# A recurrent attention and a sine MLP on one core: a list scheduler's order is made anew with other operation times

## The chip, the cores and the metric

The kernel runs on one core of a Trainium2 chip. The metric is the time of one execution on the device, in microseconds (us); smaller is better. Engines are named as in the profile: PE (TensorE, matmuls), ACT (ScalarE), DVE (VectorE), POOL (GpSimd) and SP (SyncE, which here only issues DMA transfers).

## The reference

Two stages. The first is a gated linear attention: a state of 48 x 48 per head is decayed by the gate f, takes the outer product of k and v, and is read by q. The second is an MLP over the 3072 tokens with a sine in its activation.

```python
# q, k, v, f_logit: (4, 8, 768, 48)
f = 1.0 / (1.0 + np.exp(-f_logit))
for t in range(S):
    state = f[:, :, t, :, None] * state + np.einsum('bhd,bhe->bhde', k[:, :, t], v[:, :, t])
    y[:, :, t] = np.einsum('bhd,bhde->bhe', q[:, :, t], state)
# x = y as (3072, 384); w_in (384, 2048), w_out (2048, 384)
h = x @ w_in
s = np.sin(alpha * h)
g = h + s * s / (alpha + 1e-09)
return (g @ w_out).astype(np.float32)
```

## The kernel before

**Tiling.** The sequence is cut into 6 chunks c of 128 steps. A unit u = 2c + half is one chunk of two of the four batches; each unit loads f, k, q and v (384 KB each, SP's queue, three buffers per tensor). `pre(u)` makes the gates: ACT takes exp and ln of f (L328, L331), PE adds up the logs with a triangular mask (cs, L351 and L354), ACT takes two exponentials of the sums (Gi, L364, and in place, L360), and the products with k and q become one bf16 tile qk (L373: k on POOL or DVE, q on DVE); DVE casts v (vb, L335) and keeps the decay at the chunk's end (gl, L368).

**Attention.** `attend(c, b)` works on a chunk of one batch. PE transposes qk (tp, L409) and ACT or DVE copies it out (tr, L417); for chunks 4 and 5 a DMA transpose on SP's queue does both (L415). PE makes the scores (aps, L426), DVE masks them (at, L429), PE adds the old state's part and the scores' part (y, L438 and L446), ACT or DVE casts the result (yn, L452). It is transposed into xT by PE (yt, L466, copied at L469) for chunks 0 to 2 and by a DMA on SP's queue for chunks 3 to 5 (L462). The state goes on by kv (L474, L476), sum (L482) and st (L486, POOL or DVE). All PSUM tiles of this part share three buffers (ring "a").

**MLP.** `first(c, fb)` makes a block of 128 hidden units for a chunk's 512 tokens (chunk 0: two halves of 256): three matmuls into h (L543; three PSUM buffers, in chunk 0 also the two of o), Sin on ACT (L548), the square on POOL, ACT or DVE (L556, L554), and g = h + s*s/alpha on DVE (L561), which frees h. `second(c, t)` adds up 16 matmuls into o (L581; two PSUM buffers) for the 128 tokens of one batch, copies them out (osb, L589, ACT or DVE) and stores them from SP's queue (L592). An index as in h_3_13 is chunk and block; 0' marks the second half of chunk 0.

**The order.** The instructions of all engines stand in an order that a list scheduler in the kernel's own code makes at build time (`in_order`). Every operation is an `op` with a rank, a table of engines with an assumed duration in ns, dependencies and buffers. At each step the scheduler takes the operation that could start first, and the lower rank where several could. Where an operation may run on more than one engine, a number for that engine (`BIAS`, and `ON_ACT` for ACT) is added to its start before the comparison. Ranks come from `RANK`, `ATT` and `LAG` (by unit or chunk) and `KIND` (by kind of operation). Each engine then works strictly in this order.

Some orders are fixed beside it: `LOADS` is the order of the loads on SP's queue, `W_GATE` names the loads (by place in `LOADS`) whose landing lets POOL issue the two halves of w_in and then w_out, and `PHASES` orders ACT's work: the gates use the table with exp and ln, the MLP the table with Sin, and at each change ACT loads a table (L643). So ACT runs stretches: units 0 and 1, 18 Sins, units 2 and 3, 14 Sins, units 4 and 5, 10 Sins, unit 6, 6 Sins, units 7 and 8, 16 Sins, units 9 to 11, 48 Sins.

Of the kernel before, what the change touches and what calls it, by code (L numbers as in the profile page):

```python
# [22 lines left out]
LOADS = [("f", 0), ("k", 0), ("q", 0), ("f", 1), ("q", 1), ("v", 0), ("k", 1), ("v", 1), ("q", 3),  # L23
    ("f", 2), ("v", 2), ("f", 3), ("k", 4), ("q", 2), ("k", 2), ("v", 3), ("k", 3), ("f", 4),
    ("f", 5), ("v", 4), ("q", 4), ("v", 7), ("q", 5), ("f", 7), ("k", 5), ("k", 6), ("v", 5),
    ("q", 8), ("f", 6), ("f", 8), ("q", 6), ("k", 7), ("v", 6), ("k", 8), ("v", 8), ("v", 10),
    ("v", 9), ("k", 10), ("q", 7), ("f", 10), ("v", 11), ("q", 10), ("f", 11), ("k", 9), ("q",
    9), ("k", 11), ("q", 11), ("f", 9)]
W_GATE = [4, 7, 14]
LAG = [1259, 664, 156, 107, 352, 821]  # L30
ATT = [816, -410, -264, -308, -540, 67]
# [3 lines left out]
RANK = [57, 902, -416, 116, 324, -1107, 154, -228, -393, 499, -57, -21]  # L35
MULS = {"POOL": 1020, "DVE": 750}
KIND = {"v": [-253, -197, -275, -90, -19, -113, 54, -23, 294, 108, -136, 11],
        "cs": [166, -99, 466, 468, 497, 525, 156, 73, 308, 100, -174, -211],
        "kh": [-420, -288, -109, -60, -261, -416, 1, 112, -116, -353, -597, -410],
        "qh": [39, -59, -267, -207, -95, -105, -79, -204, -36, -58, 106, 145],  # L40
        "tp": [-704, -587, -407, -250, -350, -423, -529, -434, -209, -113, -630, -619],
        "tr": [676, 683, 605, 574, 597, 434, 658, 637, 516, 502, 841, 893],
        "a": [-193, -33, -307, -268, -491, -499, -415, -297, -236, -148, -542, -369],
        "m": [382, 244, 882, 926, 455, 521, 870, 880, 558, 664, 209, 409],
        "y": [359, 281, 782, 934, 738, 726, 967, 789, 882, 759, 797, 900],
        "yt": [338, 442, 591, 498, 369, 453, 920, 776, 936, 571, 725, 839],
        "xe": [164, 118, 474, 430, 628, 568, 660, 448, 819, 638, 731, 791],
        "i": [-178, -9, -130, -85, -385, -454, -347, -676, -80, 105, -145, 51],
        "kv": [105, 140, -54, 56, 130, -66, -209, -24, 56, 108, 260, 93],
        "st": [-156, -144, -34, 68, -433, -296, -147, -222, -33, 60, -123, -22],  # L50
        "h": [-282, -193, -192, -427, -22, -104, -640, -227, -306, -284, -211, -314],
        "sq": [110, -5, -368, -360, -77, -233, -538, -538, -402, -388, -227, -18],
        "g": [-196, -86, -99, -320, -310, -185, -65, -203, 63, 30, -333, -448],
        "ev": [98, 89, -544, -601, -357, -242, -98, -190, -420, -283, -225, -463]}
ON_ACT = {"tr": [164, -107, -316, 43, -634, 114, -467, 93, 3854, -711, -8369, -5250],
          "y": [-1550, -3600, -3600, -14550, -10950, -650, 1050, -4550, -350, -5050, 3650, 100],
          "xe": [5550, 6200, -5450, 2700, 200, -100, 4250, 6900, 4000, 6850, 2600, 2800],
          "sq": [200, 900, 10400, -1400, -450, 450, -100, -1000, -250, 7250, -250, 12600],
          "ev": [7850, 12700, 3150, 2350, 850, 50, -5400, -700, 3000, 9250, 8600, -1850]}
BIAS = {"ACT": 500, "DVE": 500, "POOL": 600, "SP": 200}  # L60
# [98 lines left out]
def kernel(  # L159
# [45 lines left out]
    PE, ACT, DVE, POOL, SP = "PE", "ACT", "DVE", "POOL", "SP"  # L205
# [4 lines left out]
    EXP, TRIG = "natural_log_exp_and_others", "trig_and_small"  # L210
# [6 lines left out]
    def op(rank, engs, emit, deps=(), takes=(), holds=(), table=None, dma=None):  # L217
        o = Op(rank, engs, emit, [d for d in deps if d is not None], list(takes), table, dma)
        for b in list(takes) + list(holds):
            b.users.append(o)  # L220
        ops.append(o)
        return o

    R = {n: Ring(b) for n, b in dict(
        f=3, k=3, q=3, v=3, lf=2, qk=NQ, vb=NV, gl=6, Gi=4, a=N_A, tr=4, at0=3, at1=3, xT=2,
# [96 lines left out]
    def pre(u, rank):  # L322
# [15 lines left out]
        l = op(rank, {ACT: 790}, ln_, deps=[x], takes=[lf], holds=[fb_], table=EXP)  # L338
        act = [x, l]
        made["v", u] = op(rank + KIND["v"][u] + 2, {DVE: 870}, values, deps=[vb_.ready], takes=[vv], holds=[vb_])  # L340
        late = []
        for i in range(2):
# [34 lines left out]
            c_ = op(rank + KIND["cs"][u] + i, {PE: 170 if last else 370}, cs_, deps=[l], takes=[cb], holds=[lf])  # L377
# [8 lines left out]
            made["qh", m] = op(rank + KIND["qh"][u] + i, {DVE: 490}, qm, deps=[g, qb_.ready], takes=[qkb], holds=[qb_, cb])  # L386
            if not last:
                made["gl", m] = op(rank + i, {DVE: 110}, gl_, deps=[g], takes=[glb], holds=[cb])
# [3 lines left out]
    def attend(c, b, rank):  # L392
# [35 lines left out]
        def m_(e, r):  # L428
            nc.vector.tensor_mul(tl[x, "at", r], tl[x, "a"][r], mask4)  # L429
# [59 lines left out]
        if c < PE_TR:  # L489
            kt = op(rank + KIND["tp"][u], {PE: 250}, lambda e: tp_(e, 0), deps=[made["kh", m]], takes=[tpb], holds=[qkb])  # L490
            qt = op(rank + KIND["tp"][u], {PE: 250}, lambda e: tp_(e, 1), deps=[made["qh", m], kt], holds=[tpb, qkb])
            tr = op(rank + KIND["tr"][u], {DVE: 640, ACT: 970}, tr_, deps=[qt], takes=[trb], holds=[tpb])
            tr.on_act = ON_ACT["tr"][u]
        else:
            tr = op(rank, {SP: 1300}, tr_, deps=[made["kh", m], made["qh", m]], takes=[trb], holds=[qkb], dma=3000)
        a = op(rank + KIND["a"][u], {PE: 400}, a_, deps=[tr], takes=ab + atb, holds=[trb])
        ms = [op(rank + KIND["m"][u], {DVE: 640}, lambda e, r=r: m_(e, r), deps=[a], holds=[ab[r], atb[r]]) for r in range(2)]
        last_ = None
        if not first:
            last_ = op(rank + KIND["i"][u], {PE: 210}, inter_, deps=[a, made["st", c - 1, b]], takes=[yb], holds=[trb, sold])  # L500
        for r in range(2):
            last_ = op(rank + KIND["i"][u], {PE: 170}, lambda e, r=r: intra_(e, r), deps=[ms[r], last_, made["v", u]],
                       takes=[yb] if first and r == 0 else [], holds=[yb, atb[r], vb])
        y_op = op(rank + KIND["y"][u], {DVE: 520, ACT: 430}, y_, deps=[last_], takes=[ynb], holds=[yb])
        y_op.on_act = ON_ACT["y"][u]
        if c < Y_TR:
            yt = op(rank + KIND["yt"][u], {PE: 200}, yt_, deps=[y_op], takes=[ytb], holds=[ynb])
            made["x", c, b] = op(rank + KIND["xe"][u], {DVE: 300, ACT: 440}, x_, deps=[yt], takes=[xb], holds=[ytb])
            made["x", c, b].on_act = ON_ACT["xe"][u]
        else:  # L510
            made["x", c, b] = op(rank + KIND["xe"][u], {SP: 1300}, yt_, deps=[y_op], takes=[xb], holds=[ynb], dma=1200)
        if not last:
            sold_op = made.get(("st", c - 1, b))
            if c < SUM:
                kv = op(rank + KIND["kv"][u] + 1, {PE: 200 if first else 370}, kv_, deps=[made["kh", m], made["v", u], sold_op],
                        takes=[kvb, sb], holds=[qkb, vb] + ([sold] if sold else []))
                made["st", c, b] = op(rank + KIND["st"][u] + 1, {DVE: 520}, st_, deps=[kv, made["gl", m]],
                                      holds=[sb, kvb, bufs["gl", m]])
            else:
                kv = op(rank + KIND["kv"][u] + 1, {PE: 200}, kv_, deps=[made["kh", m], made["v", u], sold_op],  # L520
                        takes=[kvb, sumb, sb], holds=[qkb, vb])
                su = op(rank + KIND["st"][u] + 1, {DVE: 520}, sum_, deps=[kv, sold_op], holds=[sumb, kvb, sold])
                made["st", c, b] = op(rank + KIND["st"][u] + 1, {POOL: 800, DVE: 710}, st_, deps=[su, made["gl", m]],
                                      holds=[sb, sumb, bufs["gl", m]])
            bufs["st", c, b] = sb


    def first(c, fb, ts, rank, needs):
# [39 lines left out]
        s = op(rank, {ACT: 455 if half else 645}, sin_, deps=[a, made["al"]], takes=[sb], holds=[hb], table=TRIG)  # L568
        t = op(rank + KIND["sq"][w], {POOL: 640 if half else 1040, ACT: 420 if half else 640, DVE: 520 if half else 917}, sq, deps=[s], takes=[s2b], holds=[sb])
        t.on_act = ON_ACT["sq"][w]  # L570
        made["g", c, fb, ts.start] = op(rank + KIND["g"][w], {DVE: 420 if half else 685}, add, deps=[t], takes=[gb], holds=[s2b, hb])
        return s

    def second(c, t, rank):
# [18 lines left out]
        v_ = op(rank + KIND["ev"][2 * c + t // 2], {DVE: 520, ACT: 500}, ev, deps=[prev], takes=[sbuf], holds=[ob])  # L593
# [81 lines left out]
```

## Time and profile before

| | |
|---|---|
| median of 7 runs | 220.29 us (219.09 to 220.7) |
| the profiled execution, in all | 218.93 us |
| its span, first to last instruction | 217.2 us |
| busy PE / DVE / ACT / POOL | 180.9 / 160.2 / 163.4 / 100.0 us |
| mean granted TensorE clock | 0.958 |
| DMA moved | 30.30 MB |

The costliest groups of the profile, each with its operation, count, busy time, mean of one, and idle time of the engine before them:

```profile
L556 POOL TENSOR_TENSOR s<-s 128x512 f32<-128x512 f32 (+1 forms) x67 | 58.5, 888 | 67.9 <-ACT s L548 46.9
L543 PE MATMUL h<-xT,w_in_bf 128*128 128x512 bf16 (+1 forms) x336 | 78.3, 358 | 10.1 <-DMA w_in_bf<-in_moe_w_in_dram 5.3
L548 ACT ACTIVATE s<-h,al_p 128x512 f32<-128x512 f32 (+1 forms) x112 | 67.4, 626 | 25.2 <-PE h L543 21.7
L561 DVE SCALAR_TENSOR_TENSOR g<-s,al_r,h 128x512 bf16<-128x512 f32 (+1 forms) x112 | 72.0, 666 | 10.2 <-POOL s L556 6.5
L581 PE MATMUL o<-w_out_bf,g 128*128 128x384 bf16 x384 | 78.4, 329 | 0.0
```

Matmuls overlap each other, so 329 ns is how long one o matmul takes from start to end, not how far apart they stand. No engine is full over the whole span, and where each is full differs by stage; the stages are the stretches of ACT between its table loads. In the span's 40 slices each digit is a busy share in tenths, and a slice is 5.43 us.

### The profile page before, as it was taken

The numbers are of one execution on the slowest core, as the hardware profiler recorded it, in microseconds if no ns is written. First come the engines' busy times: TensorE is split into PE (matmuls) and PEld (weight loads), VectorE is DVE, ScalarE is ACT, GpSimd is POOL, SyncE is SP. The second block draws the span as 40 slices with busy tenths as digits, with TensorE's granted clock in tenths as the row PEclk, the third lists the DMA queues.
The fourth block names the chain that finished last, engine by engine and source line by source line (L and its number), as shares of the span: only waits on it lengthen the run. The fifth ranks groups of instructions, "written<-read, shape, count | busy, mean of one in ns | idle before, by whom it ended". The sixth has DMA issues, their size and how long they took to land.

```text
span 217.2 us, 4284 instructions
## 1 busy us (share of the span) xinstructions
PE 180.9 (83%) x1537; PEld 107.3 (49%) x1537; DVE 160.2 (74%) x297; ACT 163.4 (75%) x269; POOL 100.0 (46%) x129
## 2 busy tenths in 40 slices
PE   0468628546999979896999979998999999999993
PEld 0337515335676654463665535554554555555561
DVE  2386864657689589988969997759999968787820
ACT  3565535996579987798998898997898888687601
POOL 5332534767352378856675725378504213203200
PEclk9999995965899999999999999999999999999999
DMA  7999999999999999969939999586201211001121
GB/s 130 188 187 197 190 186 197 188 208 216 213 160 198 188 166 202 180 120 210 191 82 145 186 188 196 144 170 147 69 15 41 92 54 41 0 36 72 38 74 72
DMA packets 118997, 30.30 MB, mean 139 GB/s; under 512 B 113072, under 2 KB 118208, under 8 KB 118976
## 3 DMA queue, kind: packets, MB, share of 16 engines
q1 hardware_dynamic: 115968, 26.88, 71.5%
q0 software_dynamic: 3008, 3.15, 9.2%
q8 instruction: 12, 0.20, 0.4%
q14 instruction: 9, 0.07, 0.1%
HBM read 25.17 MB, written 4.72 MB: 138 GB/s over the span
## 4 chain that ended last, share of the span: by engine, by line
PE 52%; ACT 13%; DVE 9%; DMA 8%; POOL 6%; SPq 5%; issue 5%; ACTq 0%; POOLq 0%
PE o L581 23%; PE h L543 22%; SPq L270 5%; DMA v<-in_v_dram 5%; DVE g L561 4%; POOL s L556 4%; DMA w_in_bf<-in_moe_w_in_dram 3%; ACT L643 3%; ACT s L548 3%; ACT Gi L364 2%; DVE at L429 2%; PE aps L426 2%; ACT lf L331 1%; ACT f L328 1%; PE tp L409 1%
## 5 line engine op out<-in xcount | busy, mean ns | idle before, releaser
L556 POOL TENSOR_TENSOR s<-s 128x512 f32<-128x512 f32 (+1 forms) x67 | 58.5, 888 | 67.9 <-ACT s L548 46.9
L543 PE MATMUL h<-xT,w_in_bf 128*128 128x512 bf16 (+1 forms) x336 | 78.3, 358 | 10.1 <-DMA w_in_bf<-in_moe_w_in_dram 5.3
L548 ACT ACTIVATE s<-h,al_p 128x512 f32<-128x512 f32 (+1 forms) x112 | 67.4, 626 | 25.2 <-PE h L543 21.7
L561 DVE SCALAR_TENSOR_TENSOR g<-s,al_r,h 128x512 bf16<-128x512 f32 (+1 forms) x112 | 72.0, 666 | 10.2 <-POOL s L556 6.5
L581 PE MATMUL o<-w_out_bf,g 128*128 128x384 bf16 x384 | 78.4, 329 | 0.0
L543 PEld LDWEIGHTS <-w_in_bf 128*128 128x128 bf16 x336 | 32.8, 101 | 36.4 <-issue 7.5
L581 PEld LDWEIGHTS <-g 128*128 128x128 bf16 x384 | 35.7, 98 | 23.5 <-issue 0.5
L429 DVE TENSOR_TENSOR at<-aps,mask 128x512 bf16<-128x512 f32 x48 | 31.7, 684 | 4.4 <-PE aps L426 4.2
L373 POOL TENSOR_TENSOR qk<-k,Gi 128x384 bf16<-128x384 f32 x22 | 21.9, 1012 | 21.2 <-ACT Gi L364 18.8
L373 DVE TENSOR_TENSOR qk<-q,cs 128x384 bf16<-128x384 f32 x24 | 13.1, 552 | 12.8 <-ACT cs L360 12.2
L554 ACT ACTIVATE s<-s 128x512 f32<-128x512 f32 (+1 forms) x34 | 20.8, 614 | 0.9
L351 PE MATMUL cs<-lf,mask 128*128 128x384 bf16 x24 | 8.1, 357 | 9.9 <-ACT lf L331 8.5
L446 PE MATMUL y<-vb,at 128*128 128x48 bf16 x192 | 11.5, 187 | 4.9 <-DVE vb L335 3.0
L409 PE MATMUL tp<-ident,qk 128*128 128x128 bf16 x128 | 12.2, 258 | 3.3 <-POOL qk L373 1.9
L446 PEld LDWEIGHTS <-at 128*128 128x128 bf16 x192 | 8.9, 98 | 11.1 <-DVE at L429 5.2
L643 ACT ACT_TABLE_LOAD x11 | 14.1, 1283 | 0.2
L328 ACT ACTIVATE f<-f 128x768 f32<-128x768 f32 x12 | 10.1, 838 | 5.0 <-DMA f<-in_f_logit_dram 4.9
L426 PE MATMUL aps<-tr 64*128 64x128 bf16 x192 | 11.2, 230 | 2.4 <-ACT tr L417 1.5
L364 ACT ACTIVATE Gi<-cs 128x384 f32<-128x384 f32 x24 | 11.6, 485 | 1.9 <-PE cs L354 1.9
L417 ACT COPY tr<-tp 128x1024 bf16<-128x1024 bf16 x10 | 9.9, 1019 | 3.9 <-PE tp L409 3.9
L556 DVE TENSOR_TENSOR s<-s 128x512 f32<-128x512 f32 (+1 forms) x11 | 7.8, 709 | 6.8 <-ACT s L548 6.6
L409 PEld LDWEIGHTS <-qk 128*128 128x128 bf16 x128 | 10.4, 117 | 4.9 <-POOL qk L373 2.6
(54 smaller groups left out, 155.3 us busy)
## 6 DMA issues: line engine op xcount, KB each, us to landing
f<-in_f_logit_dram SPq DMA_DIRECT2D x12, 384.0 KB, 7.0
k<-in_k_dram SPq DMA_DIRECT2D x12, 384.0 KB, 6.5
q<-in_q_dram SPq DMA_DIRECT2D x12, 384.0 KB, 6.8
v<-in_v_dram SPq DMA_DIRECT2D x12, 384.0 KB, 6.8
out_dram<-osb SPq DMA_DIRECT2D x24, 192.0 KB, 2.0
w_in_bf<-in_moe_w_in_dram POOLq DMA_DIRECT2D x6, 256.0 KB, 6.6
w_out_bf<-in_moe_w_out_dram POOLq DMA_DIRECT2D x4, 384.0 KB, 6.5
xT<-yn SPq DMA_TRANSPOSE x12, 2.4
```

The lines of the kernel that those rows point to most:

```text
L364: nc.scalar.activation(out=tl["Gi", m], in_=tl["cs", m][:, :H * D], func=Act.Exp)
L373: engine[e].tensor_mul(qk_b[bufs["qk", m].place % NQ][:, "kq".index(n), :, :, :D], tl[n, u][:, i * H:(i + 1) * H, :].rearrange("c (r p) d ...
L409: nc.tensor.transpose(tl[x, "tp"][:, j * HP + p, :], qk_b[qkb.place % NQ][:, j, p, :, :].rearrange("c r e -> c (r e)"), ident)
L429: nc.vector.tensor_mul(tl[x, "at", r], tl[x, "a"][r], mask4)
L446: nc.tensor.matmul(tl[x, "y"][:, h * D:(h + 1) * D], tl[x, "at", r][:, p, :], v_b[vb.place % NV][:, i, h, :], start=(first and p == r == 0 ...
L543: nc.tensor.matmul(h[:, :n], w_in_bf[:, kb, fs], xT[:, ts.start // C:ts.stop // C, kb, :], start=(kb == 0), stop=(kb == KB - 1))
L548: nc.scalar.activation(out=s[:, :n], in_=tl[x, "h"][:, :n], func=Act.Sin, scale=al_p[:, fb:fb + 1])
L554: nc.scalar.activation(out=s2[:, :n], in_=s[:, :n], func=Act.Square)
L556: engine[e].tensor_mul(s2[:, :n], s[:, :n], s[:, :n])
L561: nc.vector.scalar_tensor_tensor(tl["g", c, fb][:, ts], tl[x, "s2"][:, :n], al_r[:, fb:fb + 1], tl[x, "h"][:, :n], Alu.mult, Alu.add)
L581: nc.tensor.matmul(tl["o", c, t], tl["g", c, fb][:, t * P:(t + 1) * P], w_out_bf[:, fb, :], start=(fb == 0), stop=(fb == FB - 1))
L643: nc.scalar.preload_act_table_set(now)
```

## The change

All durations that the scheduler assumes are set to other values, and with them all of its other numbers: the loads' order, the gates' places, the ranks and the per-engine numbers. No operation is added, removed or altered, `PHASES` stays, and the values computed stay the same. What changes is the order of the instructions on each engine and, for operations that have a choice, the engine.

```diff
-LOADS = [("f", 0), ("k", 0), ("q", 0), ("f", 1), ("q", 1), ("v", 0), ("k", 1), ("v", 1), ("q", 3),
-    ("f", 2), ("v", 2), ("f", 3), ("k", 4), ("q", 2), ("k", 2), ("v", 3), ("k", 3), ("f", 4),
-    ("f", 5), ("v", 4), ("q", 4), ("v", 7), ("q", 5), ("f", 7), ("k", 5), ("k", 6), ("v", 5),
-    ("q", 8), ("f", 6), ("f", 8), ("q", 6), ("k", 7), ("v", 6), ("k", 8), ("v", 8), ("v", 10),
-    ("v", 9), ("k", 10), ("q", 7), ("f", 10), ("v", 11), ("q", 10), ("f", 11), ("k", 9), ("q",
-    9), ("k", 11), ("q", 11), ("f", 9)]
-W_GATE = [4, 7, 14]
-LAG = [1259, 664, 156, 107, 352, 821]
-ATT = [816, -410, -264, -308, -540, 67]
+LOADS = [("f", 0), ("k", 0), ("q", 0), ("f", 1), ("v", 0), ("q", 1), ("k", 1), ("v", 1), ("f", 3),
+    ("k", 3), ("q", 3), ("f", 2), ("q", 2), ("k", 4), ("k", 2), ("v", 3), ("v", 2), ("f", 4),
+    ("q", 4), ("f", 5), ("q", 5), ("k", 5), ("v", 4), ("v", 7), ("v", 5), ("k", 6), ("f", 6),
+    ("k", 7), ("q", 8), ("f", 7), ("q", 6), ("k", 8), ("f", 8), ("v", 6), ("v", 8), ("v", 9),
+    ("v", 10), ("k", 9), ("q", 7), ("k", 10), ("f", 11), ("f", 9), ("q", 11), ("q", 9), ("q",
+    10), ("k", 11), ("f", 10), ("v", 11)]
+W_GATE = [5, 7, 14]
+LAG = [1394, 1064, 594, 47, 278, 1466]
+ATT = [814, -396, -222, -531, -395, 119]
...
-        "y": [359, 281, 782, 934, 738, 726, 967, 789, 882, 759, 797, 900],
+        "y": [-24, 45, 570, 660, 439, 417, 826, 557, 855, 722, 643, 734],
...
-BIAS = {"ACT": 500, "DVE": 500, "POOL": 600, "SP": 200}
+BIAS = {"ACT": 400, "DVE": 500, "POOL": 600, "SP": -12300}
...
-        l = op(rank, {ACT: 790}, ln_, deps=[x], takes=[lf], holds=[fb_], table=EXP)
+        l = op(rank, {ACT: 840}, ln_, deps=[x], takes=[lf], holds=[fb_], table=EXP)
...
-            tr = op(rank + KIND["tr"][u], {DVE: 640, ACT: 970}, tr_, deps=[qt], takes=[trb], holds=[tpb])
+            tr = op(rank + KIND["tr"][u], {DVE: 670, ACT: 1010}, tr_, deps=[qt], takes=[trb], holds=[tpb])
...
-        a = op(rank + KIND["a"][u], {PE: 400}, a_, deps=[tr], takes=ab + atb, holds=[trb])
+        a = op(rank + KIND["a"][u], {PE: 345}, a_, deps=[tr], takes=ab + atb, holds=[trb])
...
-        t = op(rank + KIND["sq"][w], {POOL: 640 if half else 1040, ACT: 420 if half else 640, DVE: 520 if half else 917}, sq, deps=[s], takes=[s2b], holds=[sb])
+        t = op(rank + KIND["sq"][w], {POOL: 640 if half else 1040, ACT: 420 if half else 640, DVE: 470 if half else 820}, sq, deps=[s], takes=[s2b], holds=[sb])
...
```

`RANK`, the other rows of `KIND`, all of `ON_ACT` and the remaining durations change in the same manner. The number of `BIAS` for SP has no part in any comparison, since no operation has SP beside another engine.

## The prediction

> **What bounds the kernel now.** I read the page's slices first, to see which engine is full where. The kernel alternates between two ACT tables, so I then cut the span at ACT's table loads, taken from ACT's timeline, and asked for the busy time of each engine in each piece. The waits, the chain that ended last and the SP queue came last.
>
> ```profile
> PE   0468628546999979896999979998999999999993
> DVE  2386864657689589988969997759999968787820
> ACT  3565535996579987798998898997898888687601
> 40.14:48.39 8.25, 4.10 (x37) 2.67 (x36) 3.88 (x8) 8.03 (x14) 5.22 (x8) 0.83 1.38 198
> 48.39:66.85 18.46, 16.31 (x181) 11.93 (x182) 14.57 (x31) 12.35 (x23) 10.04 (x16) 0.80 1.16 200
> 66.85:77.20 10.35, 10.35 (x104) 6.64 (x101) 7.08 (x19) 10.16 (x17) 2.74 (x5) 1.00 1.26 188
> 77.20:90.87 13.67, 11.61 (x132) 6.49 (x131) 13.22 (x22) 10.44 (x17) 12.31 (x13) 1.00 1.14 183
> 113.36:133.15 19.79, 17.96 (x146) 9.31 (x144) 18.62 (x32) 16.98 (x28) 10.65 (x12) 1.00 1.34 183
> 133.15:144.70 11.55, 11.29 (x88) 6.41 (x87) 7.52 (x15) 11.37 (x21) 6.42 (x7) 1.00 0.62 149
> 144.70:217.20 72.50, 67.66 (x461) 36.10 (x459) 53.16 (x81) 51.48 (x82) 20.21 (x21) 0.99 0.22 61
> ```
>
> Columns of the cut: stretch, length, busy PE, weight loads, DVE, ACT, POOL, clock, DMA share, GB/s. Three regimes stand out. Up to 34 us the second half of w_in is awaited. From 40 to 145 us ACT is nearly full: its gaps lie in the Sin stretches, while the Exp stretches (40 to 48, 67 to 77, 133 to 145) have none. From 149 us PE is full:
>
> ```profile
> 146.77 0.27 PE L446 MATMUL y<-vb,at 128*128 128x48 bf16 x4 [0.51 <-DVE at L429]
> 149.11 0.81 PE L543 MATMUL h<-xT,w_in_bf 128*128 128x512 bf16 x3 [0.25 <-DVE g L561]
> 204.07 9.60 PE o L581 x59
> ACT s L548 <- PE h L543: 21.7, 40, 5.0
> DVE g L561 <- POOL s L556: 6.5, 17, 1.1
> 125.60 1.97 SPq L270 DMA_DIRECT2D f<-in_f_logit_dram  x1
> 127.66 3.22 SPq L415 DMA_TRANSPOSE tr<-qk  x1
> 132.86 5.43 SPq L462 DMA_TRANSPOSE xT<-yn  x4
> ```
>
> The matmul at 149.11 is h_3_3, the fourth first-layer block of chunk 3. The chain ends with 59 matmuls in 9.60 us, so one o costs 0.163 us; three h matmuls cost 0.65 (start to start in PE's timeline). Likewise a transpose costs 0.054, a score matmul (aps) 0.042, a y or kv matmul about 0.03 to 0.042. With these, 63.6 us of PE work stand from h_3_3 on, and 213.7 - 149.1 = 64.6 us pass. So the end is the start of h_3_3 plus the PE work that is left, and h_3_3 starts 4.4 us after the last table load at 144.70. That load is set by ACT's stretches before it.
>
> **What the Trainium skill says.** "ScalarE: Activation LUTs", What ACT_TABLE_LOAD costs, gives 1283 ns for a load and a drain of about 1380 ns. The trace has 1283 ns (x11) and the next activation 10 ns later: no drain is charged. "SBUF — State Buffer", Who interferes with whom, says that a DVE cast in a two-port mode and a POOL operation block each other fully. The trace agrees: the values' cast (L335, 0.56 us at best) at 47.13 took 2.25 us while POOL ran two products. "TensorE: Matmul & The Clock Gate", What's actually happening, says that PE's clock falls to half after an idle window: the granted clock is 0.50 from 50 to 55 us, after the thin stretch from 40. "Perfetto Trace Analysis", DMA Instruction — HWDGE, says that the record of a DMA instruction ends before the data has moved: an SP load shows about 2 us, but lands 6.5 to 7.0 us after its issue.
>
> **The change, part by part.** No operation is added or removed. By the instruction order of both programs, three tr copies go from DVE to ACT (3 x 1.02 = +3.1 us ACT, 3 x 0.685 = -2.1 DVE), two k products from DVE to POOL (2 x 1.012 against 2 x 0.837), and one or two squares, xT, st and osb change sides. ACT: +0.48 (osb), +0.42 (square), -0.48 (xT); in all 171.9 to 175.4 us by row means, which count overlaps twice. DVE: about -3.0. PE's 161 us stays as it is.
>
> *0 to 40 us.* v_1 stays the eighth load, so its landing, the POOL gate behind it (23.8 us) and the landing of w_in's second half (33.9) stay. On PE kv_0_2 now stands ahead of aps_0_2 and needs v_1, so h_0_0 starts near 26.6 instead of 21.7. The eight Sins before the second half take 8 x 0.42 plus a table load and yn and end near 34: covered by that landing, but with nothing left over. After it POOL's squares set the pace (9 in 5.64 us); now 8 are POOL's and 2 ACT's, and ACT's 12 x 0.42 = 5.0 becomes the pace: -0.5 us (between 0 and -0.7).
>
> *Sin stretch from 48.* DVE takes gl_6 and a q product before the values' cast, which frees PSUM for the next transposes about 1.5 us earlier (PE waited until 50.54 for this). But 11.3 us of PE work stand between h_0_5 and h_0_15 instead of 9.5, and ACT has a tr and a yn more (12.6 to 13.2). I carry -0.5; bounds 0 and -2.
>
> *Exp stretch from 67.* Two tr and a yn leave ACT (2 x 0.97 + 0.38), two xT come in (2 x 0.38), and h_1_0 waits for these xT, the cs behind it for 0.35 us: -1.1, carried -1.6.
> *Sin stretch from 77.* Its ACT work rises from 11.1 to 12.6 us. Each Sin waits for an h, that for one of three PSUM buffers, freed by g: 10 Sins in 12.4 us. The 2.6 us of ACT gaps take part of the 1.6 us; +0.9, carried -0.7. In the short Exp stretch from 91, cs_12 stands behind h_1_12 in both orders: carried -0.5.
> *Sin stretch from 97.* POOL now has st_2_0, a product, a square, st_2_1 and only then the next squares; DVE's square there is gone. One st (0.85) comes into the loop: +0.9, carried +0.4.
> *Exp stretch from 104.* tr_3_2 leaves ACT (about -0.7), cs_15 and cs_17 come behind h_2_0 to h_2_2, which wait for the last xT_2 (+0.3): carried 0.
> *Sin stretch from 113.* ACT +0.9 (tr_3_3 and an osb in, a square out), DVE 20 us in 21 in both. Bounds -0.3 and +1.2; I take +0.5.
> *Exp stretch from 133.* A yn leaves (-0.4). But SP's order has changed: k_10, f_11, f_9, q_11, q_9, q_10, k_11, f_10 and v_11 stand in one row, and k_10 needs the buffer of k_7, free near 112. Nine loads at 2.07 us (384 KB at 185 GB/s) end at 131 to 133; before there were seven, from 113.5 to 127.6. tr_4_0 (issued at 112.2 before), tr_4_1 and two xT_3 stand behind them, so aps_4_0 starts near 136, with PE waiting up to 3 us; the cs behind it is still in time. h_3_0 then starts near 140, and 3 h, 13 o and two cs (4.4 us) stand before cs_23: the last Gi comes about 0.4 us late. Net 0 (between -0.4 and +1.8), carried +0.5.
>
> *The end.* Ahead of h_3_3 PE had 97.3 us of work; now 95.7, because 188 instead of 192 o matmuls, and one batch less of chunk 4's scores (8 matmuls) and y products (16), stand there: 4 x 0.163 + 8 x 0.042 + 0.6 = 1.6 us move behind h_3_3. From h_3_13 on both orders are the same (108.8 us of work ahead, 212 o). Between these two points before had 12.0 us for 11.5 of work; now 13.1 of work needs about 13.3: +1.3. Two st on POOL stand ahead of the first square, against a DVE wait that they replace: +0.1.
>
> Sum: +0.5 + 1.3 + 0.1 = +1.9 us on a span of 217.2. The profiled execution took 218.93 in all, 1.36 under the median of 220.29; added to both, 220.8 and 222.2.
>
> **The rivals.**
> Faster. The Exp stretch from 67 hands on its 1.1 us whole, because the lighter DVE (21.0 instead of 22.4 us up to g_1_9) lets the loop run while ACT takes the tr copies in its gaps, and the stretch from 48 gives 0.9. Then the last table load comes at -0.5 - 0.9 - 1.1 - 0.4 = -2.9; plus 1.4 at the end: -1.5 us, 218.8; with ACT's gaps closed further, 216.5. It decides once the load comes before 143.3 (144.70 - 1.4). For it: ACT idles 5.9 us in the stretch from 48 and DVE is full from 77. Against it: the three h buffers set that pace, and the tr go into the same in-order queue as the Sins.
> No change. The deferred o fall into PE's gaps before h_3_3 (0.51, 0.15, 0.25 us there) and the stretches come out even: 220.3. Against it: 1.6 us is more than these gaps.
> Slower by the load row. If k_10's buffer comes 1 us later, or the transposes drain slower, v_11's cast (ahead of g_2_13 on DVE) and aps_4_0 pass the time at which cs_18 is due, and ACT waits up to 1.8 us: 224.0.
> That the new order doesn't take effect is out: the programs differ on all five engines.
>
> **How the numbers follow.** Forecast, 221.3 to 223.2: 0.33, at 222.2. Load row, 223.2 to 226: 0.14. No change, within 1.1 us of 220.3: 0.19. Faster, 216.5 to 219.2: 0.34. Within 0.5% is about what a measurement of this kernel can't tell from no change. So faster 0.34, same 0.19, slower 0.47. Cut to four fifths, the range is 217.4 to 224.4; the likeliest case alone has 221.3 to 223.2.
>
> **What would show it.** The last table load between 144.5 and 146 and h_3_3 4.5 us behind it; about 13.3 us from h_3_3 to h_3_13; the Exp stretch from 67 shorter by a microsecond and the next Sin stretch longer; a PE wait for tr near 133. A load before 143.3 makes me wrong, as does a PE that was never full behind h_3_3.

## The result and the profile after

| | before | after |
|---|---|---|
| median of the runs | 219.77 us (57 runs, 217.35 to 221.23) | 220.46 us (22 runs, 219.33 to 222.11) |
| ratio after / before | | 1.0053, 95% interval 1.0032 to 1.0075 |
| the profiled execution | 218.93 us | 221.25 us |
| its span | 217.2 us | 219.6 us |

The ratio is taken over fast runs alone, that is without those over 1.5% above the fastest of the same kernel, which are 9 of the 57 of the kernel before and none of the kernel after. The change costs 0.7 us by the medians of all runs, and about 1.2 us (half a per cent) by the ratio. Slower was the likeliest side; the size, 222.2 us, was not met. The two profiled executions lie 2.32 us apart, twice what the ratio says. That gap has to be explained too.

The clock's row of the page's slices, first of the kernel before (a slice is 5.43 us), then of the kernel after (5.49 us); a digit is a tenth:

```profile
PEclk9999995965899999999999999999999999999999
PEclk9999999757999999976999999999999999999999
```

In both the clock falls somewhere between 38 and 60 us. The kernel before had a dip in slice 7 too (32.6 to 38 us), which is gone; the dip in slices 18 and 19 (93 to 104 us) is new. Next, the kernel after, cut at its own table loads (stretch, length, busy PE, weight loads, DVE, ACT, POOL, clock, DMA share, GB/s):

```profile
27.29:38.81 11.52, 9.32 (x72) 6.26 (x72) 9.31 (x21) 10.35 (x25) 7.79 (x13) 1.00 1.14 192
47.06:64.33 17.27, 16.33 (x190) 11.61 (x189) 14.23 (x30) 12.81 (x23) 10.22 (x16) 0.86 1.13 197
64.33:73.39 9.06, 7.86 (x64) 4.56 (x63) 5.19 (x14) 8.79 (x16) 3.79 (x4) 1.00 1.20 188
73.39:87.20 13.81, 12.40 (x143) 7.50 (x142) 12.57 (x22) 11.73 (x17) 10.57 (x12) 1.00 1.13 185
93.07:104.41 11.34, 8.64 (x77) 5.25 (x75) 9.32 (x15) 7.48 (x10) 8.43 (x9) 0.70 0.83 140
104.41:112.67 8.26, 6.17 (x62) 3.32 (x59) 6.00 (x14) 8.04 (x14) 5.01 (x6) 1.00 0.33 100
112.67:133.79 21.12, 20.11 (x156) 10.99 (x153) 19.75 (x32) 17.99 (x28) 10.07 (x10) 1.00 1.25 188
133.79:145.28 11.49, 10.74 (x82) 5.88 (x83) 7.20 (x15) 11.08 (x19) 6.00 (x7) 1.00 0.75 147
```

In the same view of the kernel before, the end of its first Sin stretch, the six Sins, and the Exp stretch behind them:

```profile
33.94:40.14 6.20, 5.54 (x28) 3.97 (x29) 4.18 (x9) 4.52 (x10) 4.37 (x8) 0.61 1.20 183
96.53:104.19 7.66, 5.96 (x63) 3.52 (x62) 6.70 (x11) 6.92 (x10) 5.37 (x6) 1.00 1.04 211
104.19:113.36 9.17, 9.17 (x103) 5.79 (x100) 7.26 (x17) 8.95 (x14) 5.98 (x7) 1.00 0.61 123
```

Set side by side, the starts of the table loads (in us) give a ledger. The last column is the forecast's carried sum.

| ACT's table load | before | after | difference | forecast |
|---|---|---|---|---|
| Exp, units 2 and 3 | 40.14 | 38.81 | -1.33 | -0.5 |
| Exp, units 4 and 5 | 66.85 | 64.33 | -2.52 | -0.5 |
| Sin (10 Sins) | 77.20 | 73.39 | -3.81 | -1.6 |
| Sin (6 Sins) | 96.53 | 93.07 | -3.46 | -0.5 |
| Exp, units 7 and 8 | 104.19 | 104.41 | +0.22 | +0.4 |
| Sin (16 Sins) | 113.36 | 112.67 | -0.69 | 0 |
| Exp, units 9 to 11 | 133.15 | 133.79 | +0.64 | +0.5 |
| Sin (last) | 144.70 | 145.28 | +0.58 | +0.5 |
| start of h_3_3 | 149.11 | 150.23 | +1.12 | +0.6 |
| end of the last o | 213.66 | 215.99 | +2.33 | +1.9 |

The last three rows are near the forecast, but the way there isn't. Up to 93 us the new order gains 3.5 us, and in the stretch of six Sins it loses 3.7. PE's timeline of the kernel after shows that place (start, duration, operation, tile, count, idle time and what ended it):

```profile
93.77 0.34 PE L466 MATMUL yt<-ident,yn 128*128 128x128 bf16 x3
96.01 0.48 PE L426 MATMUL aps<-tr 64*128 64x128 bf16 x8 [1.90 <-ACT tr L417]
97.29 1.44 PE L543 MATMUL h<-xT,w_in_bf 128*128 128x512 bf16 x3 [0.80 <-DVE g L561]
98.52 0.53 PE L581 MATMUL o<-w_out_bf,g 128*128 128x384 bf16 x1
98.84 1.06 PE L409 MATMUL tp<-ident,qk 128*128 128x128 bf16 x8
...
102.58 1.02 PE L543 MATMUL h<-xT,w_in_bf 128*128 128x512 bf16 x3
104.89 0.34 PE L581 MATMUL o<-w_out_bf,g 128*128 128x384 bf16 x1 [0.35 <-DVE g L561]
```

PE waits 1.90 us for tr_3_0, whose copy stands on ACT behind the table load and a Sin, and then 0.80 for g_1_10. From 97.3 to 102.6 matmuls take nearly twice their time (three h 1.44 us instead of 0.81, eight tp 1.06 instead of 0.61), and the granted clock of that window is 0.50. The kernel before waited for tr_3_0 too, 1.46 us, and then 0.24 for g, and its clock stayed at 1.00 (the line of 96.53). So the question was whether the fall is the loss or only comes with it.

### The profile page after: what moved, and what is told of

It is laid out like the page before. It is cut to its first block, busy times and chain, and to the rows that moved or that the text cites. A ratio compares the mean times of both kernels' runs of the same rounds, so it can differ in the third digit from the quotient of the medians.

```text
span 219.6 us, 4261 instructions
## 1 busy us (share of the span) xinstructions
PE 184.4 (84%) x1537; PEld 108.7 (50%) x1537; DVE 158.3 (72%) x293; ACT 166.7 (76%) x273; POOL 100.5 (46%) x129
## 4 chain that ended last, share of the span: by engine, by line
PE 56%; DMA 15%; DVE 9%; ACT 7%; SPq 4%; issue 4%; POOL 3%; DVEq 0%; ACTq 0%; POOLq 0%
PE h L543 24%; PE o L581 23%; DMA k<-in_k_dram 9%; SPq L270 4%; DVE g L561 4%; DMA w_in_bf<-in_moe_w_in_dram 3%; DMA w_out_bf<-in_moe_w_out_dram 3%; POOL s L556 2%; PE aps L426 2%; ACT L643 2%; PE y L446 2%; ACT s L548 2%; DVE vb L335 1%; DVE qk L373 1%; PE tp L409 1%
## 5 line engine op out<-in xcount | busy, mean ns | idle before, releaser
L556 POOL TENSOR_TENSOR s<-s 128x512 f32<-128x512 f32 (+1 forms) x66 | 57.1, 875 | 74.2 <-ACT s L548 54.1
L543 PE MATMUL h<-xT,w_in_bf 128*128 128x512 bf16 (+1 forms) x336 | 80.0, 360 | 8.1 <-DVE g L561 5.1
L373 POOL TENSOR_TENSOR qk<-k,Gi 128x384 bf16<-128x384 f32 x24 | 23.8, 1014 | 20.8 <-ACT Gi L364 19.8
L351 PE MATMUL cs<-lf,mask 128*128 128x384 bf16 x24 | 8.8, 377 | 11.0 <-ACT lf L331 9.7
L417 ACT COPY tr<-tp 128x1024 bf16<-128x1024 bf16 x13 | 13.0, 1013 | 4.9 <-PE tp L409 4.9
L368 DVE TENSOR_TENSOR gl<-cs,bd 128x8 f32<-128x8 f32 x20 | 3.2, 161 | 18.5 <-ACT cs L360 18.4
L452 ACT CAST yn<-y 128x384 bf16<-128x384 f32 x17 | 8.1, 477 | 6.7 <-PE y L446 6.6
```

The source lines that it names most:

```text
L373: engine[e].tensor_mul(qk_b[bufs["qk", m].place % NQ][:, "kq".index(n), :, :, :D], tl[n, u][:, i * H:(i + 1) * H, :].rearrange("c (r p) d ...
L543: nc.tensor.matmul(h[:, :n], w_in_bf[:, kb, fs], xT[:, ts.start // C:ts.stop // C, kb, :], start=(kb == 0), stop=(kb == KB - 1))
L556: engine[e].tensor_mul(s2[:, :n], s[:, :n], s[:, :n])
```

## The experiments

Theory A says that PE's clock, falling behind the new wait, makes the loss of the six-Sin stretch and decides how long an execution takes. Theory B says that the order of DVE and POOL there (casts of v and a state product ahead of squares) makes it. For the end the theory is the prediction's: PE is full from h_3_3 on. All repeats below write the same values once more, so nothing is left out of the computation.

Where an experiment moves an operation, the scheduler's finished order is taken, and `moved` puts one operation right ahead of or behind another; everything else stays in its place:

```diff
-    for o, e in in_order(ops, {"table": act_order, "load": load_order, "h": h_order, "cs": cs_order}):
+    todo = in_order(ops, {"table": act_order, "load": load_order, "h": h_order, "cs": cs_order})
+    for what, ahead in MOVES:
+        todo = moved(todo, what, ahead)
+    for o, e in todo:
```

**The changed kernel again (after_again).** The same kernel once more.

> The changed kernel as it is. Theory A (clock): between 93 and 104 us PE idles 1.9 and 0.8 us in front of aps_3_0 and h_1_13, and in a part of the executions its clock then falls to half for some 6 us; so the executions fall into two groups, mean clock near 0.975 with a span near 218.2 us and near 0.960 with a span near 219.6, and the median lies between, 220.1 to 220.7 us. Theory B (order of DVE and POOL): the 3.7 us lost in that stretch come from casts and state products ahead of the squares and are there in every execution; spans then don't follow the clock.

Six runs: 221.35 us median (220.14 to 222.24), above the 220.1 to 220.7 that was expected. Each execution has its mean clock on record. All executions of the two kernels that have one, sorted by it (medians in us):

| mean clock | before (168 executions, three sessions) | after (28 executions) |
|---|---|---|
| 0.972 and more | 7, median 217.4 | 11, median 219.96 |
| 0.966 to 0.971 | 16, 219.4 | 5, 220.6 |
| 0.956 to 0.965 | 86, 219.24 | 12, 221.47 |
| less | 59, 220.56 | none |

The changed kernel takes 1.5 us more where its mean clock is near 0.960 than where it is near 0.975. Both profiled executions of the kernel after (0.960) show the fall at 97. The profile of before (0.958) lies below its median by 0.84 us. The table also shows what the mean clock alone does not explain: in each of the three rows that both kernels have, the new order is the slower one, by 1.2 to 2.6 us, and it has no execution in the lowest row, where the old one has 59 of 168.

**PE kept busy in the wait (warm97).**

```diff
-            for kb in range(KB):
+            for kb in list(range(KB)) * REPEAT.get((c, b), 1):
                 nc.tensor.transpose(tl[x, "yt"][:, kb, :], tl[x, "yn"][:, kb, :], ident)
+REPEAT = {(2, 2): 12}
```

> The changed kernel with the three transposes of yt_2_2 issued 12 times instead of once (the same values written again), 33 more of 0.054 us = 1.8 us of PE work in the place where PE waited 1.90 us for tr_3_0. Theory A: the clock stays at 1.00 in that stretch, every execution has a mean clock of 0.974 or more, the stretch from the table load near 93 to the next takes about 9.3 us instead of 11.3, and the median is 0.4 to 0.9 us under that of the changed kernel. Theory B: no gain, 0 to +0.5 us.

220.01 us median (218.35 to 221.19, 22 runs), ratio to before 1.0028 (1.0004 to 1.0051). The 28 executions of the kernel after have a median of 220.62. No execution fell below a mean clock of 0.969 (theory A expected 0.974; six lie at 0.969). Its cut and PE's timeline:

```profile
93.50:102.17 8.67, 7.59 (x101) 5.42 (x101) 8.44 (x14) 7.38 (x10) 7.66 (x9) 1.00 0.70 131
102.17:111.66 9.49, 7.71 (x66) 4.02 (x66) 6.52 (x15) 8.23 (x14) 5.88 (x7) 0.82 0.52 146
```

```profile
94.20 2.18 PE L486 MATMUL yt<-ident,yn 128*128 128x128 bf16 x36
97.73 0.81 PE L574 MATMUL h<-xT,w_in_bf 128*128 128x512 bf16 x3 [0.89 <-DVE g L592]
103.70 0.34 PE L614 MATMUL o<-w_out_bf,g 128*128 128x384 bf16 x1 [0.76 <-DVE g L592]
106.28 1.44 PE L574 MATMUL h<-xT,w_in_bf 128*128 128x512 bf16 x3 [0.19 <-DVE xT L489]
```

The stretch shrinks from 11.34 to 8.67 us with the clock at 1.00: of the 3.7 us lost there, 2.7 were the clock. But the next stretch grows from 8.26 to 9.49, since now the clock falls at 106, behind waits much like those that the kernel after had there without a fall. Theory A holds for the place; the fall was moved, not removed.

**The order of DVE and POOL (order97).**

```diff
+MOVES = [(("v", 6), ("behind", ("at", 3, 0, 1))),
+         (("v", 8), ("behind", ("g", 1, 13))),
+         (("st", 2, 1), ("behind", ("sq", 1, 12)))]
```

> The changed kernel with the casts of v_6 and v_8 behind at_3_0 and g_1_13 on DVE (they stood ahead of g_1_10) and st_2_1 behind the square of h_1_12 on POOL. Theory B: the stretch from 93 gets 1 to 2 us shorter and the time falls by 0.7 us or more. Theory A: g_1_10 comes at most 0.35 us earlier, the clock still falls in a part of the executions, and the time moves by 0 to -0.4 us.

224.85 us (223.04 to 225.69, 6 runs), ratio 1.0265 (1.0207 to 1.0323): a miss for both theories. Three lines from SP's, DVE's and PE's timelines suggest why:

```profile
83.75 16.70 SPq L288 DMA_DIRECT2D v<-in_v_dram  x4
109.13 0.56 DVE L625 COPY osb<-o 128x384 f32<-128x384 f32 x1 [2.39 <-DMA out_dram<-osb]
110.01 1.44 PE L575 MATMUL h<-xT,w_in_bf 128*128 128x512 bf16 x3 [2.22 <-DVE xT L490]
```

In the kernel after the same four v loads are through in 11.63 us. The cast of v frees the buffer that a later v load waits for. Put 5 us later, it holds up SP's queue and the stores behind the loads. The copy of o then waits for a store buffer, the copy of xT stands behind it on DVE, and h_2_0 waits for xT. This chain is read from the timelines; the three moves were not made one by one. The six-Sin stretch itself was 1.2 us shorter (94.05 to 104.19), as theory B expected, but its clock was 0.83 instead of 0.70, so the run doesn't part the two theories there. It says nothing of the state product alone either.

**The state product alone (st21),** on warm2_o13 below: only the last of these three moves.

> warm2_o13 with st_2_1 behind the square of h_1_12 on POOL, alone. The prediction's step (one state product of 0.85 us in the loop of the six Sins costs 0.9): the stretch from the table load near 93, 8.7 us in warm2_o13, gets 0.4 to 0.9 us shorter, and the median falls by 0.2 to 0.8 us from 217.97. Theory A (that stretch lost its time to the clock, POOL had slack): the stretch stays within 0.2 us and the median within 0.3.

218.13 us (22 runs) against 217.97 in an earlier session; the stretch takes 8.67 us against 8.68. The state product ahead of the squares costs nothing there. What the casts cost at full clock, no run tests.

**The end (o13_early).**

```diff
+MOVES = [(("osb", 2, 2), ("before", ("sum", 4, 2)))]
+MOVES += [(("o", 1, 3, i), ("before", ("aps", 4, 1))) for i in range(5)]
+MOVES += [(("o", 1, 3, i), ("before", ("h", 3, 3))) for i in range(12, 16)]
```

> The changed kernel with the copy of o_2_2 ahead of the sums of chunk 4 on DVE, five o_1_3 matmuls ahead of aps_4_1 and the last four o_1_3 ahead of h_3_3, so that 192 and not 188 o matmuls stand ahead of h_3_3. Theory (PE is full from h_3_3 on, so what stands behind it adds its own length): 4 x 0.163 = 0.65 us plus the gaps of 0.73 and 0.47 us that are filled ahead of it, so -0.6 to -1.2 us. Rival (the loop of Sin, square and g sets the pace from 149 to 162, PE has slack there): 0 to -0.2 us.

219.69 us (22 runs), ratio to before 1.0019 (0.9993 to 1.0044), 0.77 us under the kernel after. From the last table load to the end it takes 69.95 us (145.61 to 215.56), after 70.71, before 68.96. PE's timeline there:

```profile
145.60 0.50 PE L504 MATMUL kv<-vb,qk 128*128 128x96 bf16 x8
145.94 0.98 PE L622 MATMUL o<-w_out_bf,g 128*128 128x384 bf16 x5
146.84 0.58 PE L454 MATMUL aps<-tr 64*128 64x128 bf16 x8
150.44 0.81 PE L582 MATMUL h<-xT,w_in_bf 128*128 128x512 bf16 x3
```

Five o fill what was a wait of 0.48 and 0.25 us ahead of aps_4_1, h_3_3 stays 4.8 us behind the load, and four o fewer behind it take 0.64 us off the way to h_3_13 (12.53 against 13.17). So PE's work behind h_3_3 adds its own length, as the prediction said of the end, and the rival (PE has slack there) is out.

**Both places kept busy, and all together (warm2, warm2_o13).** warm2 adds to warm97 the wait that took the fall over:

```diff
-            for p in range(HP):
+            for p in list(range(HP)) * AGAIN.get((c, b), 1):
                 for r in range(2):
+AGAIN = {(3, 1): 3}
+REPEAT = {(2, 2): 12, (2, 3): 4}
```

> The changed kernel with the filling of warm97, and also aps_3_1 issued three times instead of once (16 more of 0.042 us = 0.67) and yt_2_3 four times (9 more of 0.054 = 0.49), ahead of the waits between 102 and 106. In the profile of warm97 the clock no longer fell at 97 but at 106.3 (six h and cs there at half speed), which gave back some 1.2 us. Theory A: this fall goes too, mean clock 0.980 or more, last table load about 1 us earlier than in warm97 (143.5), median 218.6 to 219.4. Rival: the second fall was paid for by waiting ACT anyway, or the time is lost again behind 113: the median stays at 219.7 to 220.3.

> warm2 and the moved o_1_3 of o13_early in one kernel. If the two losses lie in different places they add: 0.6 to 0.8 us under warm2, 218.0 to 218.8, faster than both kernels. If the end gains only what the clock fall left it, it equals warm2.

warm2: 218.5 us (22 runs), 0.9979 (0.9955 to 1.0003). warm2_o13: 217.97 us (217.27 to 218.63, 22 runs), 0.9948 (0.9928 to 0.9969), better than either kernel as it stands. warm2, cut as above:

```profile
93.38:102.05 8.67, 7.59 (x101) 5.42 (x101) 8.44 (x14) 7.37 (x10) 7.66 (x9) 1.00 0.72 134
102.05:110.31 8.26, 7.15 (x92) 4.62 (x92) 6.55 (x15) 8.04 (x14) 5.66 (x7) 1.00 0.51 150
110.31:131.46 21.15, 20.13 (x157) 11.12 (x154) 19.39 (x32) 17.97 (x29) 10.08 (x10) 1.00 1.20 183
```

Both stretches now run at full clock, in the profile; 14 of the 22 executions have a mean clock of 0.982 or more. The last table load comes at 143.06, 2.2 us ahead of the kernel after, and all of it reaches the end (213.77 against 215.99). The clock's falls between 93 and 110 thus cost the new order some 2 us in such an execution.

**The early fall (warm3).** warm2_o13 with the same kind of repeats between 40 and 48 us:

```diff
+MORE = {(0, 20): 5, 5: 6, 6: 5}
+TWICE = {(1, 1, 1): 5}
```

> warm2_o13 with PE filled also between 40 and 48: h_0_4 of the second half issued five times, cs_5's and cs_6's large matmul six and five times, the last four transposes of tp_1_1 five times (the same values again; about 3.6 us of PE work in waits of 1.3, 0.9, 1.2 and 1 us). Theory: the clock no longer falls between 45 and 51, where some 3 us of PE work ran at half speed; the table load near 64.6 comes 0.3 to 1.3 us earlier, the median is 0.2 to 1.0 us lower than 217.97, mean clock 0.985 or more. Rival (ACT and the loads set that stretch): the median stays within 0.2 us, or rises where a repeat delays a copy.

217.72 us (22 runs), 0.9954 (0.993 to 0.9978). The mean clock of its profiled execution is 1.00, and 0.994 or more in all 22. The stretch of 14 Sins, first in warm2_o13 and then in warm3:

```profile
47.18:64.58 17.40, 16.38 (x190) 11.30 (x189) 14.13 (x30) 12.64 (x23) 10.19 (x16) 0.90 1.28 205
```

```profile
47.77:63.99 16.22, 16.07 (x206) 11.53 (x205) 14.21 (x30) 12.53 (x24) 10.15 (x16) 1.00 1.27 211
```

The stretch is 1.2 us shorter. (That it starts 0.6 later comes from ahead of the repeats: ACT's first load for Sin stands at 28.01 against 27.43.) The last o end 0.6 us earlier, 212.22 against 212.82. The medians differ by 0.25 us, which the intervals don't tell from nothing.

**The same for the kernel before (before_warm).** tp_3_1's last four transposes seven times, in front of its own 1.46 us wait near 99.

> The kernel before the change with the last four transposes of tp_3_1 issued seven times (24 more of 0.054 us = 1.3), in the place where its PE waited 1.46 us for tr_3_0 near 99. The executions of the kernel before fall into groups too: about a third at a mean clock of 0.951 or less (median 220.5), the others at 0.961 (219.2) and above. Theory: the lowest group is the clock falling behind that same wait, so it becomes rare, and the median falls by 0.2 to 0.6 us, to about 219.1 to 219.4. Rival: the lowest group falls somewhere else; its share stays near a third and the median at 219.7.

219.89 us (22 runs), ratio 1.0012 (0.9982 to 1.0041); 8 of 22 executions still had a mean clock below 0.956. A miss: with this wait filled, the lowest clock group stays as frequent as it was (59 of 168), so it comes from somewhere else. A kernel before with the thin stretch from 40 to 50 us filled too, expected at 217.1 to 217.7, was tried twice and gave no measurement. So whether the old order gains as much as the new one stays open; its 7 executions at 0.972 and more (median 217.4) hint that it does.

**The gate of w_in (gate0_v0).**

```diff
-        return op(rank, {POOL: 100}, lambda e: nc.gpsimd.tensor_copy(seen[:, i:i + 1], tl[n, u][0:1, 0, 0:1]),
+        return op(rank, {POOL: 100}, lambda e: nc.gpsimd.tensor_copy(seen[:, i:i + 1], (tl[n, u] if i else tl["v", 0])[0:1, 0, 0:1]),
```

> The changed kernel with every engine's order as it is, only the copy on POOL that opens the first half of w_in waits for v_0, the fifth load, as the fifth load opened it before, and not for q_1, the sixth. Theory: what moved the start is this gate: with it on the fifth load, v_1 comes behind the three w_in parts again, the second gate opens at 21.5 to 23.8 us instead of 19.6, the second half of w_in lands some 2 to 4 us later and the Exp table load now at 38.8 to 39.1 comes at 39.8 to 40.5; the time rises by 0.3 to 1.2 us. Rival (the order of the loads itself, not the gate): the second gate and that table load stay within 0.3 us, and the earlier first half brings 0 to -0.5 us.

220.35 us (13 runs), ratio 1.0059 (1.0029 to 1.0088), no different from the kernel after. POOL's and PE's timelines:

```profile
21.93 0.56 POOL L302 COPY seen<-v 1x1 f32<-1x1 f32 x1 [2.90 <-DMA v<-in_v_dram]
23.93 1.12 POOL L309 DMA_DIRECT2D w_in_bf<-in_moe_w_in_dram  x2
```

```profile
31.58 3.77 PE L573 MATMUL h<-xT,w_in_bf 128*128 128x256 bf16 x24 [0.45 <-DVE g L591]
```

The second gate opens 2.3 us later than in the kernel after (19.62), as expected, and still the second half of w_in lands before the h that need it: they wait for g, and the Exp load comes at 38.26, earlier than 38.81, where 39.8 to 40.5 was expected. So a gate at 21.9 costs the new order nothing. That isn't yet the 23.8 of the kernel before, which no run restores.

**A copy on DVE instead of ACT (tr33_dve),** on warm2_o13: tr_3_3 as in the kernel before.

> warm2_o13 with the copy tr_3_3 on DVE (0.67 us) and not on ACT (1.0 us), at the same place of the order, as the kernel before had it. The stretch of 16 Sins from the load near 110 took 21.1 us against 19.8 in the kernel before. If ACT's extra work sets it, it gets 0.5 to 1.0 us shorter and the median 0.4 to 1.0 us lower; if DVE, busy 19.5 of these 21 us, sets it, the median rises by 0.1 to 0.6 us.

218.36 us (22 runs), 0.4 us over warm2_o13 in its earlier session. The stretch of 16 Sins, first in warm2_o13 and then here:

```profile
110.24:131.38 21.14, 20.13 (x157) 11.13 (x154) 19.66 (x32) 17.96 (x28) 10.07 (x10) 1.00 1.19 186
110.13:131.85 21.72, 20.30 (x157) 11.12 (x154) 20.80 (x33) 17.16 (x27) 10.44 (x10) 1.00 1.21 186
```

The stretch gets 0.58 us longer as 1.1 us of busy time goes to DVE and 0.8 leaves ACT: DVE sets this stretch, and moving the copy to ACT was right.

## Why the prediction was right on the side and wrong on the size

**The step that failed most** is "*Sin stretch from 97* ... One st (0.85) comes into the loop: +0.9". The stretch lost 3.68 us. 2.7 of them are PE's clock (warm97: 8.67 us at full clock). The last 1.0 us over before's 7.66 is near the forecast's size, but st21 shows that the state product is not its cause. ACT's timeline of warm97 divides it: ACT is busy 0.46 us longer, since a copy of xT (0.50 us), of which before had none in this stretch, stands in it, and it is idle 0.55 us longer, in waits for h. The first of these h waits for g_1_10, which stands behind a cast of v on DVE. No run tests this division. The prediction knew that the clock falls behind an idle window, but used it only for the window at 50. It didn't ask whether the new order makes another: the 1.46 and 0.24 us for which PE waited at this place became 1.90 and 0.80.

**"The profiled execution took 218.93 in all, 1.36 under the median of 220.29; added to both"** is the second. The sum of +1.9 was set against one execution of before, and the measured pair gives +2.32. But the later median of before, 219.77, is only 0.84 above its profiled execution, and the one of after lies 0.79 above its own median. The clock groups in the table under after_again, 1 to 2 us apart, are wide enough for this. Which group a profile catches is not a property of the kernel that can be added to another one.

**0 to 40 us.** "v_1 stays the eighth load, so its landing, the POOL gate behind it (23.8 us) and the landing of w_in's second half (33.9) stay" was wrong: the gate opened at 19.6, h_0_0 started at 22.8 and not at 26.6, and PE waited for w_in 2.2 us instead of 5.3. The Exp load came 1.33 us earlier, not 0.5. Two differences that the profiles show are candidates, without an experiment on either. Before issued the three parts between squares at 23.93, 25.11 and 26.33, after in a row with one product between them, from 20.12 to 22.7. And before lost its clock behind its waits for w_in: from 34 to 38 us PE was busy throughout at a granted clock of 0.50 (the line of 33.94), where the kernel after has 1.00 (the line of 27.29). The prediction put the pace there down to POOL's squares, but in these 6.2 us POOL was busy for 4.37 and PE for 5.54.

**The stretches from 48 to 93.** From 47, 1.19 us shorter, where 0 was taken and 0 to 2 allowed. Exp from 64, 1.29 shorter (forecast 1.1): right. Sin from 73, +0.14 (forecast +0.9): ACT's gaps took in nearly all of its additional work (busy 11.73 us instead of 10.44). Exp from 87, +0.21 (+0.2): right. So the rival "faster" was right that the gains are handed on whole, up to 93.

**From 104.** Exp -0.91 (forecast -0.4). Sin from 113 +1.33, above its bounds (-0.3 to +1.2; +0.5 taken); DVE sets it (tr33_dve), busy 19.75 us there instead of 18.62, and not ACT's 0.9 us. Exp from 133 -0.06 (0). PE did not wait for tr near 133: the nine loads ran from 111.48 to 128.4, not to 131 to 133, since each took 1.88 us on average and not 2.07 (384 KB at 185 GB/s would even be 2.13, with 1024 bytes in a KB). The wait that the rival "slower by the load row" named did come, for the cast of v_11 at 132.75, but it was 0.82 us long and not 1.8.

**The end** was right: h_3_3 to h_3_13 took 13.17 us (forecast 13.3), and o13_early took away what its matmuls weigh. Only the way to h_3_3 was mis-sized: it starts 4.95 us behind the load and not 4.5, with waits of 0.48 and 0.25 us ahead of aps_4_1. The break-even held too: warm2's last load at 143.06 gives an end at 213.77, equal to before's 213.66, where "a load before 143.3" was the point from which the change would be faster.

So it was luck that the +0.5 at the last load came near the measured +0.58: two errors cancel, 3 us of gains not seen and 2.8 of loss in one stretch not seen. With the waits between 93 and 106 filled, the changed kernel is level with the kernel before as it stands or a little under it (0.9979, 0.9955 to 1.0003); the kernel before with its own falls taken out was not measured.

## What to carry to other kernels

Where a reordering puts waits of PE close together in the middle of its work (here 1.90 and 0.80 us), price not only the waits but matmuls at half speed for several microseconds behind them. The mean clock of every execution tells whether it happens, and the profile tells where. Work that is there anyway, or a repeat of a matmul that writes the same values again, can be cheaper in the wait than the wait, but look where the clock falls next. Before moving a cast, ask which load waits for the buffer that it frees, and what is queued behind that load. And before adding a forecast to a median, ask in which clock group the profiled execution lies.

## What the runs showed of the hardware

The clock's fall isn't fixed by the program: of 28 executions of the same changed kernel 11 had a mean clock of 0.972 or more and 12 of 0.956 to 0.965. In the profile it followed waits of 1.90 and 0.80 us within 3.2 us, and lasted from 97.3 to 102.6. In gate0_v0 waits of 1.90 and 0.89 us at the same place were followed by half speed for 2.7 us only. When that place was filled (warm97), the clock fell at 106, behind waits of 0.76, 0.27, 0.21, 0.27 and 0.19 us within 3.4 us. But in the kernel after, waits of 0.35, 0.26, 0.42 and 0.79 us within 2.9 us from 104.5 on were not followed by a fall (clock 1.00 up to 112.67). 33 transposes that compute nothing new took 2.7 us off the stretch in which they stand.

"TensorE: Matmul & The Clock Gate" in the Trainium skill, The HAM clock gate (the "warmup" mystery), has the clock fall after an idle window of about 3.4 us that runs free of the program, so that the same kernel can differ from run to run. The spread over the executions here agrees with that. But it was no unbroken idle: PE worked 0.48 us between the two waits at 94 and 97, and the waits at 103 to 106 are a chain of short ones.
